# Sharing the first and last score columns of sliding-window attention in five tiles of the last layer, splitting the last tile's value products, and a new planned order

## The chip, the cores and the metric

The kernel runs on one core of one Trainium2 chip. The metric is the device time of one execution in microseconds (us), taken as the median of several runs. Five engines work side by side, each through its own queue in order: PE (TensorE, matrix products into PSUM), ACT (ScalarE, here the exponentials and some copies), DVE (VectorE, elementwise work), POOL (GpSimd, small work and some masks) and SP (SyncE, which issues DMAs). Semaphores join them.

## The reference: four layers, two kinds

`x` has 2048 tokens of width 512. Layers alternate: A (linear attention), B (causal attention over a window of 256 keys), A, B. Each adds its result to `x`. Heads: 32 of width 16. Cut to what matters here, the B layer is:

```python
scores = einsum("bhqd,bhkd->bhqk", q, k) * 16 ** -0.5
idx = arange(2048)
mask = (idx[:, None] - idx[None, :] >= 0) & (idx[:, None] - idx[None, :] < 256)
p = softmax(where(mask, scores, -1e9))
o = einsum("bhqk,bhkd->bhqd", p, v)
x = x + o.reshape(B, S, D) @ wo
```

A key at position n is seen by the queries n to n + 255 and no other.

## The kernel before: tiles, blocks of keys, and an order out of a table

All work is cut into 16 tiles of 128 tokens, numbered 0 to 15 (the change's "tiles ten to fourteen" are numbers 9 to 13). The program first records every operation with what it reads and writes (class `Plan`); then `place` takes the order of all operations, the engine of those that could run on either of two, and the PSUM bank of each result from a packed table (`TABLE`). So nothing is scheduled at run time: each engine runs its part of that list in order, and waits where a result or a bank isn't ready. Stages: layer 1 (A), layer 2 (B), layer 3 (A) and layer 4 (B); the code calls B's passes `middle(2)` and `middle(3)`, and interleaves the end of one layer with the start of the next.

In a B layer a tile j of keys is two blocks, b = 0 and 1, of 64 keys. Keys lie on the partitions of a score tile (64 keys times 2 heads = 128 partitions), queries on its columns. A block of 64 keys meets 64 + 255 queries, held in 320 columns:

- columns 0 to 255 are made by `b_scores` (line 617): eight matmuls for two head groups f (line 634) into four PSUM banks, then two exponentials on ACT of 128x1024 elements (line 644, one per pair of banks), then a causal mask on the first 64 columns on DVE (line 652);
- columns 256 to 319 are made by `b_far` (line 708) for all head groups of the tile at once: 32 matmuls of 64 columns (line 723), two exponentials of 128x1024 (line 732), and by `far_masks` (line 695) two masks, each on POOL (line 703) or on DVE (line 704).

So a tile takes ten exponentials of 1024 columns; tiles 14 and 15 have no far columns and fewer near ones, as the queries end. `b_values` (line 738) multiplies the probabilities with the values: 24 matmuls per head group (line 753), six blocks of keys for each of four, after the last block that reaches the tile. DVE divides by the sums (lines 765 and 766), the result is transposed, by a DMA or in the last tile by PE (line 789), multiplied with `wo` (line 400, last tile 800), added to `x` (line 568, last tile 806) and written out. The projections q, k and v of tile j + 3 are moved out of PSUM by ACT or DVE as the table says (`bqe`, `bve` at line 389, `bke` at 585 and 586).

A PSUM bank is held until its last reader is done. A group of scores needs four of the eight banks; usually two of them are freed by the first exponential of the group before, and the matmuls run while ACT works on that group's second.

The method `b_edge` (line 660), which does the shared columns, and the set `PACK` are in the kernel before already, with `PACK` empty.

Of the kernel before, what the change touches and what calls it, by code (L numbers as in the profile page):

```python
# [214 lines left out]
LATE = 5  # L215
KEEP = 6
MASKS = 0
PACK = {}
QUAD = ()
SUMMED = ()  # L220
FILL = 10
# [7 lines left out]
class Plan:  # L229
# [508 lines left out]
    def b_values(self, j, h, key):  # L738
        K = self
        rp = self.rp  # L740
        ps = Tile(1, K.cls)
        blocks = [(2 * j, 0), (2 * j + 1, -64), (2 * j - 1, 64), (2 * j - 2, 128), (2 * j - 3, 192), (2 * j - 4, 256)]
        blocks = [(b, c) for b, c in blocks if b >= 0]
        reads = []
        for f in (2 * h, 2 * h + 1):
            def put(e, f=f):
                m = None
                for gq in range(4):
                    r = 4 * f + gq
                    u = 4 * (f - 2 * h) + gq  # L750
                    for i, (b, c) in enumerate(blocks):
                        o = 384 * (b % 2) + c
                        m = e.matmul(K.ps(ps)[:, 34 * u:34 * u + 34], K.P((b // 2) % rp)[:, gq, f, o:o + P], K.vB[:, (b // 2) % 4, b % 2, r, :], start=i == 0, stop=i == len(blocks) - 1)  # L753
                return m
            rd = []
            for i in range(max(0, j - 2), j + 1):
                rd += [("P", i % K.rp, f)] + [("vB", i % 4, a, b) for a in range(2) for b in range(2)]
                rd += [("P", i % K.rp, f, b, h_) for h_ in range(3) for b in (0, 1)]
            rd += [("A", i % K.rp) for i in range(max(0, j - 2), j + 1)]
            if j >= 2:  # L760
                rd += [("F", (j - 2) % K.rp, h_) for h_ in (0, 1)] + [("F", (j - 2) % K.rp, h_, 1) for h_ in (0, 1)]
            self.pe("pv", put, key - 0.001 * (f % 2), 4 * len(blocks), 34, rd=rd, ps=[ps])
        s = j % 2
# [49 lines left out]
    def middle(self, ph):  # L813
        K = self
# [9 lines left out]
        self.packed = PACK.get(ph, ())  # L824
        if last:
# [59 lines left out]
    r"q*|$7s?a*Wo~3T8S1PT(rNZdAdWFiZPN~}}oerXQtJ5mI-lf87)baEk6;9t(XH*7Fy0I#tU#pC|pk_T=WzuKW9Cc3_{YJ&tqKByjx`2AChN~v3rY@-7sS)bF",
    r"s-;J&@cO+fq$B9kYLxn@N~nlBvo5TQ=t%m5imbEfggUEsDv{2ntxl}7>nJ*jE~=C2LaLZ{y0}iJE2|PZs!py;>Iy1{4z5b+e5$rCtb(bEx{l7N>*?XTk}j>A",
    r">&m){uA)|{7P_jgrbp=Nx`uA4SF5_Zl4_;bsHVD|ZmgT>J*u2)qZ{fby1s6$%d5Srfj+0!sz$o4KCddOeQKm$r$*`h>VlfBtE<s^j=rc4=`p&b`lPC=HF~U`",
    r"s}JjO`m>s+$Lj}bf_|tDsEK;MKBC*}NqT`^t1qdAdYWFOzo_YYonEXTsmZ#7e&c57y?TmXuV?Cxx|9B@rs`RGgWjh*>y7%d-mkmp<$9BTtXAmFdWn9bw&<05",
    r"ss5&}=w-UA4gy#8QGG)Pg=_kj?xu^uDt$~BhhT71AJ+%;6CFgK&`<SAy;YZhQ+k_zrh~%{9aJCG+x2t3Q<sEb`nrChcj?tSD!kOuAOr;0r644n)*<vOeMX0Z",
    r"(hwT%=;&}(hk<jthPtQE>xb@wzN@?IG7t}X=!^OkB!JVfN0)`_@LI=*a&QJ>K@GUAW5WoD2{mCP#DV*|HY9_D@J7GYF(5fS(C_p^Jqj-A6gmZ@)Q|LT9T&>O",  # L890
    r"d!0%@)~TQZeATISY8VY+Asmc>G>}G*g$NKHB0@zN2X$aPoP|U%0qQ~}hy;nD9-M=ox)!v6^N<88LsDo37hon_gjtXhT0&a*rY}Ji_^xL|1NfoSK_f^HKlN>B",
    r"2(96R&HxJP!ySkW8b0ZaFcI!Tc9;YJA9Wj;440uDTmgi}Ku|`1(QTouz6zNj3Y62Ibq>e^)gUJ{fvS)TGDB0C2hAWG<c2A*0H#8D&5#G?Lj|1|3^a#mS|A@R",
    r"ghh}QrolB>4A&t)SSSGPA-cW+OP~Wd=m;_NQdk9@Af{dhYhVt<(#v5kbcWT?ORs>Quo8Ofb+7^Y>4H!Q`s(!%2K(r+xE2b-6W9o^-7_cxn;;x+hNAEk!s7?1",
    r"h#%oORKhK=6?(xZsEoVe0Yt#wPz4`CM9ii8z<tQABjF?H3teCu&VZ_zM@Pon*bg2<6zm3Zu|MS1(=ng!3IiY>R>OgC2WQ|Qh>z9r4b;Fr&>h~wUbqK$u?O_m",
    r"@1Q2`gKaQCZ-*B!9bUp`*a5fTJ?w{McoV)r3OoR>;42)2*RTtc<4jD1QE{M7g5Mw-?u73!7@{L$VjKeLa3~ytx|k5tV+<Syvv4@X#MzhuQ(`8ZgGsR-X2w)l",
    r"A5&u%jD^kdFtos|SPPFpMy!o#uqCF&)>sD#+aO~ryocGaEgJj**)a~z#h=g!6JQQ(j5$%EU}roEO|T0tN5E!y47#Gm6__8pqs8OU4qv#H*dBZ0JiL!5paVX@",
    r"lh6YluEE&Y5er}t?1byEAojwC_|gT%ZnzeM;Rbw!y|EB(#6Gwln_^*n<u>7C%!Ng;FD}BO*bj5#V%&@ku^7(B;+O}Q;0`Q-3vd^{!G-u1^WjcxfP-{!9IS_6",
    r"UVMikaF~AULgF4AqE}-A+KZvEBo5W3a36-ogw!8P<4|0R1F#GZ!$h<SpWr|&i_7pSCZ;3!47cELJc?U!HzuJGcnp)$S8Ph#a6cxa@7Rn+Vsd(p%_#*9#&7rn",
    r"4`2&=iKFl%wxl0;5I^H~9F41J5FWx$xS9^*7(~iQt!OMVWun%UlG+f_8v1~#C=GqV%ybeB39Y5nbR5%?rJwj7(~+WA=;#EtrEH|>6awX-(>M;Z(-|C(K`0kZ",
# [194 lines left out]
```

## Time and profile before

| what | value |
|---|---|
| median of 3 runs | 417.3 us |
| lowest and highest | 416.35 and 420.33 us |
| the profiled execution, its own time | 415.97 us |
| its span | 414.2 us |
| mean granted TensorE clock | 0.999 of full speed |
| busy share of PE, DVE, ACT, POOL | 94%, 84%, 83%, 28% |

The page of the profile gives the busy time of each engine over the span, the busy share in 40 slices, the DMA queues, the chain of work that ended last, and groups of like instructions. A share over the whole span is a mean over stages with different limits; so the stages are looked at one by one. "ACT pb L644" is an instruction of ACT that writes the tile pb and was issued at line 644. `pb` and `vp` hold the probabilities of different tiles.

### The profile page before, as it was taken

The numbers are of one execution on the slowest core, as the hardware profiler recorded it, in microseconds if no ns is written. First come the engines' busy times: TensorE is split into PE (matmuls) and PEld (weight loads), VectorE is DVE, ScalarE is ACT, GpSimd is POOL, SyncE is SP. The second block draws the span as 40 slices with busy tenths as digits, with TensorE's granted clock in tenths as the row PEclk, the third lists the DMA queues.
The fourth block names the chain that finished last, engine by engine and source line by source line (L and its number), as shares of the span: only waits on it lengthen the run. The fifth ranks groups of instructions, "written<-read, shape, count | busy, mean of one in ns | idle before, by whom it ended". The sixth has DMA issues, their size and how long they took to land.

```text
span 414.2 us, 17130 instructions
## 1 busy us (share of the span) xinstructions
PE 387.9 (94%) x7481; PEld 258.5 (62%) x7555; DVE 346.8 (84%) x803; ACT 345.8 (83%) x432; POOL 117.7 (28%) x211
## 2 busy tenths in 40 slices
PE   7999999999999999999999999999999989988886
PEld 3545676766575577565666777586757745556554
DVE  5997898989989988778978689989799687776575
ACT  2624449998999999999997245999999999999992
POOL 4784833111241243230112302220132215230111
PEclk9999999999999999999999999999999999999999
DMA  7545316632233624444213100353306623273361
GB/s 246 177 79 148 104 40 119 131 92 68 64 96 78 110 73 113 80 107 106 56 29 69 26 2 27 93 148 79 81 7 134 137 56 95 60 159 96 93 121 54
DMA packets 67555, 37.83 MB, mean 91 GB/s; under 512 B 48248, under 2 KB 62584, under 8 KB 67480
## 3 DMA queue, kind: packets, MB, share of 16 engines
q1 hardware_dynamic: 67040, 35.54, 36.7%
q8 instruction: 60, 0.98, 1.0%
q0 software_dynamic: 432, 1.18, 0.9%
q14 instruction: 15, 0.12, 0.1%
q10 hardware_dynamic: 8, 0.00, 0.0%
HBM read 6.29 MB, written 2.10 MB: 20 GB/s over the span
## 4 chain that ended last, share of the span: by engine, by line
PE 48%; ACT 35%; DVE 9%; DMA 5%; issue 2%; SPq 1%
ACT pb L644 22%; PE ps L400 17%; PE ps L414 13%; PE ps L753 7%; ACT pb L732 6%; ACT vp L644 5%; PE ps L634 5%; PE ps L475 2%; DMA XQ<-xn 2%; DVE stats L361 2%; DMA xres<-in_A_x_dram 2%; DVE xres L568 1%; DVE XQ L557 1%; PE ps L723 1%; ACT vp L732 1%
## 5 line engine op out<-in xcount | busy, mean ns | idle before, releaser
L644 ACT ACTIVATE pb<-ps 128x1024 bf16<-128x1024 f32 (+2 forms) x224 | 206.7, 1042 | 4.5 <-PE ps L634 3.7
L753 PEld LDWEIGHTS ps<-vB,pb 128*128 128x128 bf16 x2560 | 77.5, 96 | 11.7 <-issue 4.6
L753 PE MATMUL ps<-vB,pb 128*128 128x34 bf16 x2560 | 83.2, 177 | 1.1 <-ACT pb L644 0.6
L414 PE MATMUL ps<-xT,wBp 128*128 128x128 bf16 x1024 | 69.2, 219 | 1.2 <-DVE vp L586 0.5
L414 PEld LDWEIGHTS ps<-xT,wBp 128*128 128x128 bf16 x1024 | 59.2, 98 | 13.6 <-issue 4.4
L423 ACT ACTIVATE tE<-ps 128x512 bf16<-128x512 f32 x64 | 38.5, 612 | 34.3 <-PE ps L400 15.5
L363 POOL TENSOR_SCALAR ve<-mv 128x1 f32<-128x1 f32 x64 | 16.7, 261 | 172.6 <-DVE mv L362 170.5
L634 PE MATMUL ps<-XQ,kB 32*128 32x256 bf16 (+2 forms) x1024 | 49.6, 267 | 5.0 <-ACT vp L644 1.4
L732 ACT ACTIVATE pb<-ps 128x1024 bf16<-128x1024 f32 x50 | 49.6, 1066 | 0.4 <-PE ps L723 0.2
L568 DVE TENSOR_TENSOR xres<-ps,xres 128x512 bf16<-128x512 f32 x63 | 43.1, 685 | 7.6 <-PE ps L400 7.0
L400 PE MATMUL ps<-wA,XQ 128*128 128x512 bf16 x176 | 46.2, 379 | 2.7 <-issue 0.6
L652 DVE TENSOR_TENSOR pb<-pb,tri 128x512 bf16<-128x512 bf16 x112 | 44.7, 412 | 4.0 <-ACT pb L644 3.7
L703 POOL TENSOR_SCALAR_AFFINE_SELECT pb<-pb 128x1024 bf16<-128x1024 bf16 x26 | 29.8, 1148 | 62.9 <-DVE pb L652 32.6
L361 DVE BATCH_NORM_STATS2 stats<-xres 128x6 f32<-128x512 bf16 x64 | 43.6, 686 | 2.6 <-DMA xres<-in_A_x_dram 1.8
L364 POOL TENSOR_TENSOR rs<-ve,negh 128x1 f32<-128x1 f32 x64 | 37.8, 591 | 5.3
L634 PEld LDWEIGHTS ps<-XQ,kB 32*128 32x128 bf16 x1024 | 15.5, 92 | 33.6 <-ACT pb L644 9.2
L414 PE MATMUL ps<-XQ,wA 128*128 128x128 bf16 x512 | 34.7, 219 | 0.3 <-DVE o L766 0.3
L414 PEld LDWEIGHTS ps<-XQ,wA 128*128 128x128 bf16 x512 | 30.4, 98 | 5.7 <-DVE o L766 0.6
L400 PE MATMUL ps<-wBv,xT 128*128 128x512 bf16 x112 | 31.5, 380 | 2.2 <-issue 1.3
L400 PE MATMUL ps<-wBo,oT 128*128 128x512 bf16 x105 | 28.8, 380 | 4.2 <-issue 1.1
L400 PE MATMUL ps<-M,XQ 128*128 128x512 bf16 x112 | 30.7, 380 | 2.1 <-issue 1.0
L765 DVE RECIPROCAL rc<-ps 128x16 f32<-128x16 f32 x64 | 16.1, 252 | 19.3 <-PE ps L753 19.0
(110 smaller groups left out, 532.8 us busy)
## 6 DMA issues: line engine op xcount, KB each, us to landing
vB<-vS SPq DMA_DIRECT2D x64, 136.0 KB, 2.6
kB<-vp SPq DMA_DIRECT2D x64, 128.0 KB, 2.7
wA<-in_A_wqkv_dram SPq DMA_DIRECT2D x3, 512.0 KB, 4.6
out_dram<-xres POOLq DMA_DIRECT2D x9, 128.0 KB, 2.8
xres<-in_A_x_dram SPq DMA_DIRECT2D x2, 512.0 KB, 4.3
pb<-in_B_wqkv_dram SPq DMA_DIRECT2D x1, 1024.0 KB, 5.6
xres<-in_A_x_dram SPq DMA_DIRECT2D x3, 256.0 KB, 4.8
out_dram<-xres SPq DMA_DIRECT2D x6, 128.0 KB, 2.4
```

Of the source, the lines that this page charges most:

```text
L361: self.on("DVE", "stats", lambda e: e.bn_stats(K.stats[:, t, :], K.xres[:, t, :]), key, dve(512), rd=[("xres", t)], wr=[("stats", t)])
L364: self.pow = self.on("POOL", "pow", lambda e: e.tensor_tensor(K.rs[:, t, :], K.ve[:, t, :], K.negh[:], ALU.pow), key + 0.03, (640, 690), r ...
L400: m = e.matmul(K.ps(ps), lhs(c), rhs(c), start=c == 0, stop=c == 3)
L414: m = e.matmul(K.ps(ps)[:, f * P:(f + 1) * P], w(c, f), xT(c), start=c == 0, stop=c == 3)
L423: self.on("ACT", "E", lambda e: e.activation(K.tE[:, s, :], K.ps(ps), ACT.Exp, bias=0.0), key, act(512), wr=[("tE", s)], ps=[ps])
L568: self.on("DVE", "res", lambda e: e.tensor_tensor(K.xres[:, t, :], K.ps(po), K.xres[:, t, :], ALU.add), key, dve(512), rd=[("xres", t)], w ...
L634: m = e.matmul(K.ps(ps[gq])[:, ns * i:ns * i + ns], K.kB[rows, j % 4, 2 * f + b, :, :], K.XQ[rows, f, q:q + ns], start=True, stop=True, ti ...
L644: return e.activation(out(2 * h, 2, ns), i, ACT.Exp, bias=0.0, scale=0.25)
L652: return e.tensor_tensor(x, x, K.tri[:, 0, sh:64].unsqueeze(1).unsqueeze(1).to_broadcast([P, 4, n, 64 - sh]), ALU.mult)
L703: return e.affine_select(out=x, in_=x, compare_op=ALU.is_ge, fill=0.0, base=-2, pattern=[[0, 16], [-2, 64]], channel_multiplier=1)
L732: return e.activation(far(h), i, ACT.Exp, bias=0.0, scale=0.25)
L753: m = e.matmul(K.ps(ps)[:, 34 * u:34 * u + 34], K.P((b // 2) % rp)[:, gq, f, o:o + P], K.vB[:, (b // 2) % 4, b % 2, r, :], start=i == 0, s ...
```

## The change

1. In the last layer, for tiles 9 to 13 (`PACK = {3: [9, 10, 11, 12, 13]}`), `b_scores` starts its 256 columns at 32 instead of 0, so it makes columns 32 to 287, and its mask covers 32 columns (operation `md`). `b_edge` takes the place of `b_far`: it computes columns 0 to 31 and 288 to 319 of both blocks. Only the first 32 keys of a block can meet the first 32 columns, and only the last 32 the last ones; so DVE copies partitions 64 to 127 of the last columns over the first ones, inside PSUM (`gc`, two copies of 512 elements), ACT takes exponentials of 128x512 elements twice instead of 128x1024, and DVE writes the first columns' part back to its place under a mask (`ma`, 64 partitions of 1024). The two far masks stay, on columns 256 to 319.
2. In the last tile (`SPLIT = {3: (15,)}`) the 24 value matmuls of each head group are recorded as two operations: 16 on earlier blocks of keys (`pu`) and 8 on the tile's own two blocks (`pv`).
3. A new `TABLE`: order, engines and banks of all operations in all layers. `HALF` is empty, so the third form in `b_values` (`ph`) isn't built.

```diff
-MASKS = 0
-PACK = {}
+PACK = {3: [9, 10, 11, 12, 13]}
+HALF = {}
+SPLIT = {3: (15,)}
...
-        blocks = [(2 * j, 0), (2 * j + 1, -64), (2 * j - 1, 64), (2 * j - 2, 128), (2 * j - 3, 192), (2 * j - 4, 256)]
+        blocks = [(2 * j, 0), (2 * j - 1, 64), (2 * j - 2, 128), (2 * j - 3, 192)]
+        ends = [(2 * j - 4, 256), (2 * j + 1, -64)]
+        apart = j in self.halves
+        if not apart:
+            blocks += ends
...
+        early = j in self.split
+        if early:
+            blocks = [x for x in blocks if x[1] <= 0]
+            before = [(2 * j - 1, 64), (2 * j - 2, 128), (2 * j - 3, 192), (2 * j - 4, 256)]
+            for f in (2 * h, 2 * h + 1):
...
+                self.pe("pu", put, key - 0.002 - 0.001 * (f % 2), 16, 34, rd=reads([f], before), ps=[ps])
...
 TABLE = (
...
```

`b_edge`, which now runs, is unchanged but first used:

```python
for h in range(2):
    two = ps[2 * h:2 * h + 2]
    side = lambda c, two=two: bass_view(K.PS[64:128, two[0].banks[0], c:c + 32], [[512 * (two[1].banks[0] - two[0].banks[0]), 2], [64, 8], [1, 32]])
    self.on("DVE", "gc", lambda e, side=side: e.tensor_copy(side(0), side(32)), key, dve(512), ps=two)
    def ex(e, h=h, two=two):
        return e.activation(edge(h), K.pair(two, [[128, 4], [64, 2], [1, 32]]), ACT.Exp, bias=0.0, scale=0.25)
...
def ma(e):
    x = lambda c: bass_view(K.P(sl)[0:64, 0, 0, c:c + 32], [[704, 16], [384, 2], [1, 32]])
    return e.tensor_tensor(x(0), x(288), K.tri[0:64, 0, 0:32].unsqueeze(1).unsqueeze(1).to_broadcast([64, 16, 2, 32]), ALU.mult)
```

What the new table moves, by operation counts. ACT to DVE: four evictions of v in layer 2 and one of q in layer 4, and one transposed tile in layers 1 and 2 each. DVE to ACT: two Gram-matrix evictions between layers 1 and 2, and one transposed half tile at the very end. Far masks on POOL: 15 to 19 in layer 4 and 14 to 15 in layer 2; on DVE 13 to 9 and 14 to 13. The counts of DMAs on SP and POOL stay.

In the list of layer 4, what each group of shared columns waits for is this. In tiles 9, 10 and 12 its banks come free with the first exponential of the pair just ahead on ACT's queue, so one exponential of 1024 columns runs while the group is made; in tiles 11 and 13 two do. In tile 15 the first group's banks are those of the last exponential of tile 14, and the third group's those of the exponential just ahead: none runs meanwhile there. In the table before, every group of the last eight tiles has one running. In layer 2 there are three groups with none before and six after (tile 8, tile 13's far columns and two more in tile 15 are new; tile 13 before had another).

More of the change, by code (lines that the diff above doesn't have):

```diff
@@ L215 @@
 LATE = 5
+MASKS = 0
 KEEP = 6
-MASKS = 0
-PACK = {}
+PACK = {3: [9, 10, 11, 12, 13]}
 QUAD = ()
 SUMMED = ()
+HALF = {}
+SPLIT = {3: (15,)}
 FILL = 10
@@ L824, in middle @@
         self.packed = PACK.get(ph, ())
+        self.halves = HALF.get(ph, ())
+        self.split = SPLIT.get(ph, ())
         if last:
@@ L885 @@
[L885 to L892, printed above, removed]
@@ new lines @@
+    r"t9PkeDwH~@rmGOTw5p+ls#B__zO81cGU|@1sCKHEDx^NG(&$k7m71l_sI)q?j;Hgedn$~ct@5g{`n5`@jn1dvDAeh7ejQ)GRd-bZO*(@fs@|!BdYH<oSZCB9",
+    r"l<48=y(*-`=@F{19;p)O{3^Vzr2|wY6+tJ|PDRw2bRr!|7f_kC)roZ$T|_6*1yxa<RY%svbT(Z`CDl$B*HLr{T}~y_Ido-JO4ru8RArrA*VScJC0$ZC)5TN;",
+    r"T~V)8<yCWCMOW3;^e|mrx6rFp9o<r|R>O4@-9|UkP4#ZIM%B}e^;%U$omKU91KmoWQ`J;M-B#~WBXn!MS5;6W^?7w)jncF9Y&}|kRCDwvHAe4KtMyzxRzFY|",
+    r")Hr=m&(q`ee0@moR}=IaeONEh6LoRbPCrx&^(4JkFVa(Wdp%80))&=uy+<F>9rRv3MbFUdbVt2U&(w?cBeh<4(fjohy+JS2o%B+@Q7_je)MvFxU(%iRX1zjR",
@@ L934 @@
+    r"L{}j5e)qkCrNA-`%ozkulh;JXmu(D8lD|$oWIroJ6qtT*slNq&Mh9PCiGP`w6MvBg#^y!rZ;QZqe3j#`L$4<SE7Nbs-!~pI1jgZ8?%jB4^0$#Mcy0WdQ{eOA",
+    r"e*h25L~Q",
 )
```

135 lines of the change are left out of this document (78 added, 57 removed).

## The prediction

> **What bounds the kernel now.** I read the page first, then busy time by stage, then the chain of waits of the last 75 us.
>
> ```profile
> span 414.2 us, 17130 instructions
> PE 387.9 (94%) x7481; PEld 258.5 (62%) x7555; DVE 346.8 (84%) x803; ACT 345.8 (83%) x432; POOL 117.7 (28%) x211
> PE 48%; ACT 35%; DVE 9%; DMA 5%; issue 2%; SPq 1%
> ```
>
> By the whole span PE seems to be the limit. The stages say otherwise. In the columns stand PE, its weight loads, DVE, ACT and POOL, each busy time with its count, then the granted clock (full almost throughout).
>
> ```profile
> 63.00:222.00 159.00, 152.16 (x3140) 101.26 (x3170) 139.15 (x327) 155.06 (x184) 37.81 (x67) 1.00 0.40 88
> 222.00:265.00 43.00, 42.08 (x660) 30.23 (x660) 37.53 (x83) 23.42 (x41) 9.90 (x18) 1.00 0.14 33
> 265.00:402.80 137.80, 126.92 (x2921) 86.63 (x2942) 108.84 (x247) 136.31 (x155) 31.74 (x47) 1.00 0.42 97
> 402.80:406.30 3.50, 3.50 (x108) 2.56 (x107) 3.12 (x9) 3.36 (x9) 0.54 (x1) 1.00 0.23 77
> 406.30:414.20 7.90, 3.83 (x83) 2.68 (x80) 3.41 (x10) 0.39 (x1) 0.54 (x1) 0.96 0.20 53
> ```
>
> In the two sliding-window layers, 63 to 222 and 265 to 402.8, ACT works 155.06 of 159 us and 136.31 of 137.8. The chain and ACT's longest waits confirm it: from 347 to 400 nothing but ACT stands in the chain, and ACT hardly waited.
>
> ```profile
> 346.97 12.84 ACT pb L644 x14
> 379.99 14.24 ACT pb L644 x16
> 397.90 1.83 ACT pb L732 x2
> ACT vp L644 <- PE ps L634: 0.6, 1, 0.6
> ACT pb L644 <- PE ps L634: 2.8, 8, 0.6
> ```
>
> (The fourth row is from 265 to 403, the last from 63 to 222: eight waits of 2.8 us in all.) So in these stages a microsecond off ACT ends the kernel one earlier, as long as PE and DVE keep delivering; 222 to 265, where ACT works 23.42 of 43, is not priced by it.
>
> **The change, part by part.** The prices of single instructions (columns: busy time of the group, mean ns of one); the first seven rows are ACT's, and its first row is from 63 to 222:
>
> ```profile
> L389 ACT ACTIVATE vS<-ps 128x512 bf16<-128x512 f32 x7 | 5.0, 708 | 0.0
> L732 ACT ACTIVATE pb<-ps 128x1024 bf16<-128x1024 f32 x22 | 21.9, 1075 | 0.1
> L732 ACT ACTIVATE vp<-ps 128x1024 bf16<-128x1024 f32 x6 | 5.8, 1036 | 0.1
> L644 ACT ACTIVATE vp<-ps 128x512 bf16<-128x512 f32 x4 | 2.1, 594 | 0.1
> L389 ACT ACTIVATE XQ<-ps 128x512 bf16<-128x512 f32 x2 | 1.2, 607 | 0.2 <-PE ps L414 0.2
> 376.22 1.94 ACT L644 ACTIVATE pb<-ps 128x1024 bf16<-128x1024 f32 x2
> 378.04 1.95 ACT L732 ACTIVATE vp<-ps 128x1024 bf16<-128x1024 f32 x2
> L652 DVE TENSOR_TENSOR pb<-pb,tri 128x512 bf16<-128x512 bf16 x22 | 8.6, 412 | 0.0
> L704 DVE TENSOR_TENSOR pb<-pb,tri 128x1024 bf16<-128x1024 bf16 x7 | 4.8, 687 | 0.3 <-ACT pb L732 0.3
> L389 DVE CAST vS<-ps 128x512 bf16<-128x512 f32 x6 | 4.1, 691 | 0.8 <-PE ps L400 0.8
> L703 POOL TENSOR_SCALAR_AFFINE_SELECT pb<-pb 128x1024 bf16<-128x1024 bf16 x4 | 4.6, 1152 | 1.7 <-DVE pb L652 1.5
> ```
>
> *Exponentials saved.* Two of ACT's run 1.94 us, yet the next starts 1.82 after the first: one follows another every 0.91 us and overlaps it by 0.12. The undisturbed 1036 ns row against the 594 ns row of 512 columns gives 0.44 us each; ten instructions (five tiles, two each) save 4.4 us on ACT.
>
> *The copies, and what they put in ACT's way.* Now a group of shared columns runs PE, DVE, ACT instead of PE, ACT. The times of that chain:
>
> ```profile
> 375.76 0.12 PEld L634 LDWEIGHTS ps<-XQ,kB 32*128 32x128 bf16 x8 [0.42 <-ACT vp L644]
> 377.51 0.41 PE L723 MATMUL ps<-XQ,kB 32*128 32x64 bf16 x32
> 379.12 0.12 PEld L634 LDWEIGHTS ps<-XQ,kB 32*128 32x128 bf16 x8 [0.22 <-ACT vp L732]
> ```
>
> The first L732 starts at 378.04, lasts some 1.03, and PE starts the group that waits for its banks at 379.12: 0.05 for the handover. Scores begun at 375.76 reach ACT at 376.22, shared columns begun at 377.51 at 378.04: 0.46 to 0.53. Count from the start of the exponential that frees the banks, with one more behind it (tiles 9, 10, 12): it ends at 1.03, PE starts at 1.08, DVE some 0.49 later at 1.57, the copy takes 0.69, ACT could start at 2.31, but is free at 1.82: 0.49 lost. The second copy ends 0.6 later, while ACT's short first exponential steps on after 0.47: 0.14 more. Together 0.65 per tile, 2.0 for three. In tiles 11 and 13 two exponentials (until 2.73) cover the copies; there only the next group of scores is late, as its cover is now a short instruction: 0.59 + 0.05 + 0.46 = 1.10 after the first short one starts, where ACT is done after 0.94. That is 0.16, 0.3 for both. Sum: +2.2 us. No copy from PSUM to PSUM stands in the trace. From below the 256-element divide bounds it (0.42 us, row at the tail), from above ACT's 1036 ns of twice the elements; I take the 691 ns cast, equal in elements and source. At the lower end the first copies gain 3 x 0.27 and the second cost nothing more (3 x 0.14): -1.2. At the upper end both copies of three tiles lose 0.35 each, and the second ones of tiles 11 and 13 also come late by 0.37: +2.8.
>
> *DVE and POOL.* A shared tile adds two copies (1.38) and the masked write-back of 1024 elements (0.69), and its four masks halve in columns, 0.41 to about 0.28, which the two mask rows give by their slope: +1.5 us, 7.7 for five. Four far masks go from DVE to POOL, -2.7 there and +4.6 here. Cover: DVE is idle 29 of 137.8 us, POOL 106. Priced at nothing; without the cover each is a delay of a copy, see the rivals. Behind a waiting copy stand DVE's evictions of q, k and v; who waits for those are the projections' DMAs, three tiles ahead. No DMA is added, and the output DMAs moved on SP and POOL come up long before the last rows.
>
> *The last tile's scores.* Its first group now waits for the last exponential of tile 14.
>
> ```profile
> 400.97 2.01 ACT L644 ACTIVATE pb<-ps 128x1024 bf16<-128x1024 f32 x2
> 402.12 0.24 PE L634 MATMUL ps<-XQ,kB 32*128 32x64 bf16 x8
> 402.78 3.50 ACT L644 ACTIVATE vp<-ps 128x256 bf16<-128x256 f32 x8
> 403.31 0.29 PE L634 MATMUL ps<-XQ,kB 32*128 32x128 bf16 x8
> 403.65 0.60 ACT L644 ACTIVATE vp<-ps 128x512 bf16<-128x512 f32 x1
> 403.58 0.77 PE L753 MATMUL ps<-vB,pb 128*128 128x34 bf16 x24
> 405.96 0.78 DVE L652 TENSOR_TENSOR vp<-vp,tri 128x512 bf16<-128x512 bf16 x2
> 407.17 0.42 DVE L766 TENSOR_TENSOR o<-ps,rc 128x256 bf16<-128x256 f32 x1
> 408.20 0.26 DVE L765 RECIPROCAL rc<-ps 128x16 f32<-128x16 f32 x1 [0.61 <-PE ps L753]
> ```
>
> Before, PE began it at 402.12 and ACT took it without a stop at 402.78, 0.20 ahead of its predecessor's end at 402.98. Now it can start 0.05 after that end, and 0.34 go by from PE's start to ACT's (403.31 to 403.65): 0.6 lost. The third group has no cover either, and stands on PE behind two value products (24 matmuls in 0.77 each): 0.5. Sum +1.1; 0.4 if PE is early, 1.6 if the products come late.
>
> *The last value products.* After the last mask (406.74) PE still had 48 of them before the reciprocal at 408.20. Now 32 of these run from the last exponential's end (402.78 + 3.50 = 406.28) under the mask, some 0.9 us at 24 in 0.67 (0.77 less the last one's latency), and 16 remain, 0.45: done at 407.7, so -0.5. Without this nothing else is late: the output products of tile 14 stand ahead, and their DMA lands earlier.
>
> *Layer 4's eviction.* One q goes from ACT to DVE: 607 ns less the overlap, -0.5.
>
> *Layer 2.* Four evictions of v leave ACT: 4 x (0.708 - 0.12) = -2.4; three more groups of scores have no exponential running while they are made, and the trace's waits of that kind reach 0.6: 3 x 0.5 = +1.5. Sum -0.9, between -2.4 (PE is early) and +0.6 (DVE, 88% busy here, delivers late).
>
> *The rest.* Other orders up to 63 us and from 222 to 265: the same work, two copies changed engine each way. No row favours a sign; zero, 1.5 either way.
>
> The sum: -4.4 + 2.2 + 1.1 - 0.5 - 0.5 - 0.9 = -3.0. The profiled execution took 415.97 us (span 414.2 and 1.8 around it): 413.0. It is 1.3 below the median, 417.3, and 0.4 below the lowest timed run; I leave the forecast at its level.
>
> [...] The copies start at partition 64, all else at 0. [...]
>
> **The rivals.**
>
> *The copies wait in DVE's queue.* DVE runs in order, with 0.69 us instructions about. Half of one ahead of each tile's first copy is 5 x 0.35 = 1.7, and layer 2 gains nothing (+0.9): 415.6. For it: DVE's load in the packed tiles rises by 1.5 us in each 9. Against: its idle time.
>
> *POOL's masks shut DVE's out.* If a select on POOL and a two-input mask on DVE exclude each other, a mask ahead of a copy waits up to 1.15 us: five tiles, 5.8, so 418.8. For it: eight of the ten far masks of shared tiles are on POOL. Against: most copies stand behind evictions, which read one tensor. [...]
>
> *Slower.* Every copy comes late by a whole queue: an eviction (0.69) and a mask (0.41) ahead of each of ten, and the four PSUM banks stay held meanwhile, so nothing else feeds ACT: 10 x 1.1 = 11 over the sum, 424. It decides from 0.85 us a copy, where 421.5 is passed. For it: the copies share the queue with evictions that wait for DMAs. Against: two of five tiles have 0.9 us to spare.
>
> *Better.* PE and DVE run ahead: the last tile loses 0.4 (-0.7), layer 2 keeps 2.4 (-1.5), the first stages give 1.5: 409.3. For it: only one wait over 0.5 in layer 4 before.
>
> That the change doesn't do what it says is excluded by the order: ten exponentials are of 512 columns.
>
> **How the numbers follow.** About 1% (4.2 us of 417.3) is what a measurement of this kernel can tell from no change: 413.1 and 421.5. The forecast, 413.0, lies at the lower edge; its own range is 411 to 414.3, of which 2.1 of 3.3 us lie below 413.1. Chances: forecast 0.46, better 0.18, queue 0.16, masks 0.04, slower 0.16. So of the forecast's 0.28 count as faster: faster 0.28 + 0.18 = 0.46; within 1% 0.18 + 0.16 + 0.04 = 0.38; slower 0.16. The range runs from a little below the better case to the masks' case, 408.8 to 418.8, and leaves out the slower case and some 0.04 of the better one.
>
> **What would show it.** Ten L734 rows of 128x512 near 0.59 us; copies of 0.69; ACT idle before the first shared exponential of tiles 9, 10 and 12 by about 0.5, and in 11 and 13 by none; ACT idle at the start of tile 15 by 0.4 to 0.6 twice; from ACT's last exponential to the end 7.4 us, not 7.9; ACT's busy time in layer 2 lower by 2.4 and the stage by 0.9. It is wrong if the first shared copies start more than 0.3 after their matmuls end, or if the stage from 222 to 265 or the first 63 us move by more than 1.5.

## The result, and the profile after

| | median of the runs | lowest to highest |
|---|---|---|
| before | 417.36 us | 416.01 to 420.33 |
| after | 415.86 us | 414.39 to 417.21 |

The ratio is 0.9962, 95% interval 0.9945 to 0.9979: faster by 1.5 us or 0.4%, within 1%. The forecast was 413.0, a fall of 3.0 us against the profiled execution and 4.3 against the median. Its range, 408.8 to 418.8, holds the time, but it would hold no change as well; the size of the fall does not stand. Executions whose mean granted clock is 0.996 or less take some 3 us longer (median 420.1 beside 416.9), 27 of 170 of the kernel before in the comparisons below and none of 32 of the changed kernel, so a part of the difference between the medians may lie there; without them the second comparison of the two (e13, below) has 0.85 us instead of 0.96.

The page of the changed kernel, span, busy times and the chain by engine:

```profile
span 415.4 us, 17157 instructions
PE 388.2 (93%) x7480; PEld 259.6 (62%) x7555; DVE 354.6 (85%) x817; ACT 341.3 (82%) x428; POOL 122.6 (30%) x216
PE 50%; DVE 21%; ACT 21%; DMA 3%; issue 3%; POOL 2%; POOLq 0%; DVEq 0%
```

ACT had 35% of the chain and has 21%; most of what it gave up went to DVE (9% to 21%). This execution took 417.21 us, the longest of the runs of after, while that of before took 415.97, shorter than any other. So the two traces differ by +1.2 us where the medians differ by -1.5, and their ends can't be compared; stages can. The same stretches as in the prediction (PE, weight loads, DVE, ACT, POOL):

```profile
63.00:222.00 159.00, 151.86 (x3134) 100.79 (x3168) 141.28 (x326) 152.53 (x180) 41.05 (x69) 1.00 0.39 90
222.00:265.00 43.00, 41.24 (x652) 29.93 (x657) 38.30 (x86) 21.90 (x39) 8.03 (x18) 1.00 0.13 33
265.00:402.80 137.80, 125.80 (x2890) 86.63 (x2911) 113.45 (x258) 134.47 (x154) 36.82 (x51) 1.00 0.39 95
402.80:406.30 3.50, 3.50 (x122) 3.02 (x122) 2.21 (x6) 2.33 (x5) 0.00 (x0) 1.00 0.52 120
406.30:414.20 7.90, 5.26 (x108) 3.45 (x106) 5.26 (x14) 2.51 (x6) 0.54 (x1) 1.00 0.30 85
```

In layer 2 (first row) ACT works 2.5 us less, as forecast, and waits instead. Its waits, the first three from 265 to 403, the last from 63 to 222 (where it was 2.8 in eight):

```profile
ACT pb L687 <- DVE ps L684: 1.1, 3, 0.4
ACT vp L646 <- PE ps L636: 0.8, 2, 0.6
ACT pb L646 <- PE ps L636: 0.3, 1, 0.3
...
ACT pb L646 <- PE ps L636: 3.2, 10, 0.6
```

L687 are the shared exponentials, L684 the copies. The new instructions (busy time, mean ns of one) cost what was put down for them, 705 beside 691 and 601 to 618 beside 594:

```profile
L684 DVE COPY ps<-ps 64x512 f32<-64x512 f32 x10 | 6.6, 705 | 1.4 <-PE ps L676 1.3
L687 ACT ACTIVATE pb<-ps 128x512 bf16<-128x512 f32 x8 | 4.7, 618 | 1.2 <-DVE ps L684 1.1
L687 ACT ACTIVATE vp<-ps 128x512 bf16<-128x512 f32 x2 | 1.1, 601 | 0.0
```

The timeline, on DVE at the copies of tile 10 and then at tile 12 (start, length, and in brackets the idle time before):

```profile
362.94 1.32 DVE L684 COPY ps<-ps 64x512 f32<-64x512 f32 x2
364.29 0.42 DVE L798 TENSOR_TENSOR o<-ps,rc 128x256 bf16<-128x256 f32 x1
...
381.00 2.00 ACT L646 ACTIVATE pb<-ps 128x1024 bf16<-128x1024 f32 x2
382.14 0.41 PE L676 MATMUL ps<-XQ,kB 32*128 32x64 bf16 x32
382.63 1.31 DVE L684 COPY ps<-ps 64x512 f32<-64x512 f32 x2 [0.46 <-PE ps L676]
383.38 1.20 ACT L687 ACTIVATE pb<-ps 128x512 bf16<-128x512 f32 x2 [0.38 <-DVE ps L684]
384.48 1.02 ACT L646 ACTIVATE pb<-ps 128x1024 bf16<-128x1024 f32 x1
```

PE ends at 382.55, DVE starts 0.08 later (0.08 in tiles 9, 10 and 13 too, 0.16 in tile 11): the copies don't stand in DVE's queue. ACT is idle 0.38 us before the first shared exponential, and without its usual overlap: from the start of the exponential just ahead to that of the shared one 1.47 us go by in tile 12 (381.91 to 383.38, the second of the two at 381.00), 1.60 in 9 and 1.45 in 10, where 0.90 is usual.

For the experiments I use lengths inside one trace, since most repeat to 0.2 us where whole times scatter by several; each length below is that of one trace. Spans are read to 0.1 us, so a tail is good to 0.05. "Tail" is the time from the start of tile 9's first exponential over block 0 (352.25 us before, 354.09 after) to the span's end, in three parts: to tile 15's first exponential, to the end of its last, to the end.

| run | parts | tail |
|---|---|---|
| before (three traces) | 50.53, 3.50, 7.92 | 61.95 (61.99, 62.02) |
| after (two traces) | 49.84, 4.24, 7.23 | 61.31 (61.46) |
| e1 late order only | 49.69, 4.24, 7.19 | 61.12 |
| e3 no sharing | 51.52, 4.24, 7.19 | 62.95 |
| e4 no copies | 48.66, 4.24, 7.18 | 60.08 |
| e7 no split | 49.82, 4.23, 7.82 | 61.87 |
| e8 cover in tile 15 | 49.06, 3.51, 9.00 | 61.57 |
| e9 direct scores | 50.64, 4.24, 7.20 | 62.08 |
| e14 two tiles | 50.63, 4.24, 7.26 | 62.13 |
| e15 cover in tile 12 | 50.02, 4.24, 7.22 | 61.48 |
| e16 both covers, first form | 49.42, 3.51, 9.02 | 61.95 |
| e17 tile 12, queue in order | 49.51, 4.24, 7.19 | 60.94 |
| e18 both covers, second form | 48.80, 3.51, 9.59 | 61.90 |

(The other traces of before are those of e6 and e5 below, which have its order here; the second of after is e13's. Four more traces have the order of before in the tail. e10's is 62.04, like the three. e2's is 62.44, with a last part of 8.18; e12's 62.74, with one of 8.72; e11's 64.21, with a granted clock of 0.99 from 265 to 402.8 us, where e10 and e12 have 1.00.) Against the four that agree the change wins 0.5 to 0.7 us in the tail, in e1's trace 0.8 to 0.9. All seven average 62.5, and the three with the change's late order 61.3: by these it is 1.2.

### The profile page after: what moved, and what is told of

Same layout as the page of the kernel before. It is cut to its first block, busy times and chain, and to the rows that moved or that the text cites. A ratio compares the mean times of both kernels' runs of the same rounds, so it can differ in the third digit from the quotient of the medians.

```text
span 415.4 us, 17157 instructions
## 1 busy us (share of the span) xinstructions
PE 388.2 (93%) x7480; PEld 259.6 (62%) x7555; DVE 354.6 (85%) x817; ACT 341.3 (82%) x428; POOL 122.6 (30%) x216
## 4 chain that ended last, share of the span: by engine, by line
PE 50%; DVE 21%; ACT 21%; DMA 3%; issue 3%; POOL 2%; POOLq 0%; DVEq 0%
PE ps L402 17%; ACT pb L646 13%; PE ps L416 12%; PE ps L783 9%; PE ps L636 5%; ACT pb L734 3%; DVE stats L363 3%; ACT vp L646 3%; DVE vp L427 2%; DVE xres L570 2%; DVE XQ L559 2%; DVE XQ L427 2%; DMA XQ<-xn 2%; DVE tE L426 1%; PE ps L477 1%
## 5 line engine op out<-in xcount | busy, mean ns | idle before, releaser
L646 ACT ACTIVATE pb<-ps 128x1024 bf16<-128x1024 f32 (+2 forms) x224 | 207.0, 1024 | 7.5 <-PE ps L636 6.4
L783 PEld LDWEIGHTS ps<-vB,pb 128*128 128x128 bf16 x2496 | 75.9, 96 | 12.7 <-DVE pb L654 2.9
L783 PE MATMUL ps<-vB,pb 128*128 128x34 bf16 x2496 | 81.3, 177 | 0.5 <-DVE mv L364 0.3
L705 POOL TENSOR_SCALAR_AFFINE_SELECT pb<-pb 128x1024 bf16<-128x1024 bf16 x29 | 33.2, 1145 | 59.2 <-DVE pb L654 19.4
L654 DVE TENSOR_TENSOR pb<-pb,tri 128x512 bf16<-128x512 bf16 (+1 forms) x112 | 43.8, 399 | 4.7 <-ACT pb L646 4.1
L734 ACT ACTIVATE pb<-ps 128x1024 bf16<-128x1024 f32 x42 | 41.4, 1057 | 1.1 <-PE ps L725 1.1
L416 PE MATMUL ps<-XQ,wA 128*128 128x128 bf16 x512 | 36.2, 219 | 0.4 <-ACT pb L646 0.3
L402 PE MATMUL ps<-wBv,xT 128*128 128x512 bf16 x108 | 30.3, 380 | 3.4 <-issue 1.6
L646 ACT ACTIVATE vp<-ps 128x1024 bf16<-128x1024 f32 (+2 forms) x32 | 26.8, 910 | 2.2 <-PE ps L636 2.1
```

The source lines that it names most:

```text
L402: m = e.matmul(K.ps(ps), lhs(c), rhs(c), start=c == 0, stop=c == 3)
L416: m = e.matmul(K.ps(ps)[:, f * P:(f + 1) * P], w(c, f), xT(c), start=c == 0, stop=c == 3)
L646: return e.activation(out(2 * h, 2, ns), i, ACT.Exp, bias=0.0, scale=0.25)
L654: return e.tensor_tensor(x, x, K.tri[:, 0, sh:64].unsqueeze(1).unsqueeze(1).to_broadcast([P, 4, n, 64 - sh]), ALU.mult)
L705: return e.affine_select(out=x, in_=x, compare_op=ALU.is_ge, fill=0.0, base=-2, pattern=[[0, 16], [-2, 64]], channel_multiplier=1)
L734: return e.activation(far(h), i, ACT.Exp, bias=0.0, scale=0.25)
```

## The experiments

My theory after the two traces: in the packed tiles ACT is the limit and the copies and lost cover hand back most of the saving; in layer 2 ACT is only one of several limits. The rival: the premise holds everywhere, and one trace misled me. Edits to the planned order are shown as the order of instructions.

**Which half of the kernel.** e1: the order of before until tile 9 of the last layer, then that of the change.

```diff
 order of before, entries 0 to 2223
-order of before, the rest;  PACK = {}, SPLIT = {}
+order of the change, the rest;  PACK = {3: [9, ... 13]}, SPLIT = {3: (15,)}
```

> The order of the kernel before up to tile 8's end of the last layer, and from tile 9's first scores on everything of the changed kernel: shared columns, split value products, new order. Theory (the two traces hold: the packed tiles cost what they save, 54.03 us before against 54.08 after, and the stretch behind the last exponential gains 0.7): 0.6 us under the kernel before, 416.8 beside 417.4. Rival (the whole measured gain of 1.5 us comes from these tiles, and the one trace is an unlucky run): 415.9. Forecast's own sum for this part: -4.4 + 2.2 + 1.1 - 0.5 = -1.6, so 415.8.

Measured 415.94 us beside 417.31, ratio 0.9972 (0.9937 to 1.0006); tail 61.12. e2 is the other half, cut in the middle of tile 8.

> The other half: the changed kernel's order up to the middle of tile 8 of the last layer, then the kernel before, nothing shared and nothing split. Theory (the rest of the measured -1.5 us lies here): 0.9 us under the kernel before, 416.5. Rival (these orders give nothing): 417.4. Second rival (the trace of after, which stands 1.8 us late at tile 9, is typical): 419.2.

Measured 418.22, ratio 1.0008 (0.9979 to 1.0038). In its trace 93.6 us lie between the last layer's first exponential and tile 9's, more than in any other trace (91.6 to 93.0), so it says only that the early orders bring no large gain: its interval leaves room for 0.9 us. By e1 the gain lies in the late part, though e1's interval just holds no change.

**Sharing, with and without its copies.** e3 takes the sharing out and leaves the order; e4 leaves only the copies out.

```diff
-PACK = {3: [9, 10, 11, 12, 13]}
+PACK = {}
```

> The changed kernel in its own order, without sharing: the ten exponentials have 1024 columns again, the ten copies and the five combining masks are gone, the masks have their full width. Theory (ACT is the limit in these tiles, so what the trace shows per instruction is what counts): 3.5 us of exponentials come back and 1.65 us of waits and lost cover go (three times 0.55), so 1.9 over the changed kernel, 417.7 beside its 415.9. Rival (PE and DVE would have ended no earlier, so shorter exponentials save nothing): 415.9, the same as the changed kernel.

Measured 417.85, ratio 0.9990 (0.9958 to 1.0022); tail 62.95. Sharing is worth 62.95 - 61.31 = 1.64 us (1.49 against the second trace).

```diff
-            self.on("DVE", "gc", lambda e, side=side: e.tensor_copy(side(0), side(32)), key, dve(512), ps=two)
```

> The changed kernel with the ten PSUM copies left out, so that the upper half of the shared columns holds other scores than it should; the exponentials are as short as in the change, and wait for PE alone. Theory (the copies put 0.5 us of waiting ahead of tiles 9, 10 and 12 and 0.15 more behind, nothing that another wait would take over): 1.6 to 1.9 us under the changed kernel, 414.1. Rival (the time returns as a wait for PE or for DVE's masks): 415.5 or more, within 0.4 of the changed kernel.

Measured 414.56, ratio 0.9943 (0.9914 to 0.9972); tail 60.08. Without copies the ten short exponentials give 62.95 - 60.08 = 2.87 us, and the copies take 1.23 of it (1.38 against the second trace).

**Layer 2.** e5 moves the four evictions alone.

```diff
-bve[layer 2: tiles 2, 4, 9, 10] on ACT
+bve[layer 2: tiles 2, 4, 9, 10] on DVE
```

> The kernel before, and in it only the four evictions of v of tiles 2, 4, 9 and 10 of layer 2 moved from ACT to DVE, as the change has them; order, banks and all else as before. The forecast's step (ACT is the limit in layer 2, so 4 x (0.708 - 0.12) goes): 2.4 us under the kernel before, 414.9 beside 417.3. Rival, formed from the trace of the changed kernel, in which ACT's freed time turned up as waits for PE: PE (152 of 159 us) and DVE (139, rising by 2.8) hold the layer together with ACT, and nothing is gained: 417 to 418.

Measured 418.17 beside 416.76, ratio 1.0034 (1.0014 to 1.0055): nothing gained, if anything lost. e6 was to shorten ten exponentials there.

> The kernel before, with ten of layer 2's far exponentials (tiles 9 to 13, two each) cut to 512 columns, so that the second half of their columns is left as an earlier tile had it; nothing is put in their place. This is the change's saving without its copies, in the other layer. If ACT is the limit there as it is in layer 4: 10 x 0.44 = 4.4 us under the kernel before, 412.9. Rival (PE or DVE is as late as ACT): under 1.5 us of it arrives, 416 or more.

Its edit did nothing: it chose the layer by a setting that is already the last layer's when instructions are written out, and all exponentials kept their length. So 416.60, ratio 1.0012 (0.9991 to 1.0033), is the kernel before once more. e10 is the same with the choice made in time. e11 instead leaves out the two farthest of the six blocks of keys in the value products of the same tiles, and e12 does both.

```diff
+w = 32 if self.rp == 3 and 9 <= j <= 13 else 64
-i = pair(ps[2 * h:2 * h + 2], [[128, 4], [64, 2], [1, 64]])
+i = pair(ps[2 * h:2 * h + 2], [[128, 4], [64, 2], [1, w]])
```

> The kernel before, with ten of layer 2's far exponentials (tiles 9 to 13, two each) really cut to 512 columns, the second half of their columns left as an earlier tile had it, and nothing put in their place: the change's saving without its copies, in the other layer. If ACT is the limit there, as its 155 of 159 us say: 10 x 0.43 = 4.3 us under the kernel before, 412.6 beside 416.9. Rival (PE, 152 of 159 us, is as late as ACT): under 2 us of it arrives, 415 or more.

```diff
+if self.rp == 3 and 9 <= j <= 13:
+    blocks = blocks[:4]
```

> The kernel before, with the value products of the same five tiles of layer 2 cut from six blocks of keys to four (the two farthest are left out), 5 x 4 x 8 matmuls less, some 0.2 us for each of 20 groups, 4 us of PE in all; ACT has all its work. If ACT is the limit in layer 2: nothing, 416.9. Rival (PE is the limit there): 3 to 4 us under the kernel before, 413.5. If both hold each other: 1 to 2 us.

> Both cuts of layer 2 together, 4.3 us of ACT and 4 us of PE. If either engine alone is the limit: the same as the run that cuts that engine. If the two are co-limits, so that each cut alone is taken up by the other engine: 3.5 to 4.3 us under the kernel before, 413, and more than the two cuts give one by one.

| run | time, ratio | from tile 2's first exponential to layer 2's last (starts) |
|---|---|---|
| before, e6, e1 (same order) | | 144.01, 144.15, 144.30 us |
| e5, evictions | 418.17 | 144.44 |
| e10, ACT 4 us less | 416.79, 0.9998 (0.9979 to 1.0018) | 143.79 |
| e11, PE 3 us less | 417.75, 1.0015 (0.9989 to 1.0040) | 143.69 |
| e12, both | 417.61, 1.0003 (0.9975 to 1.0031) | 143.40 |

Some 4 us off ACT bring 0.4, some 3 off PE 0.5, both 0.8 (against 144.15, the middle of the three, which differ by 0.3). The trace shows where it goes. The kernel before, timeline of ACT and of SP's queue:

```profile
71.97 1.36 SPq L594 DMA_DIRECT2D kB<-vp  x2
...
81.09 3.77 ACT L644 ACTIVATE pb<-ps 128x1024 bf16<-128x1024 f32 x4 [0.24 <-PE ps L634]
...
174.97 1.03 ACT L732 ACTIVATE pb<-ps 128x1024 bf16<-128x1024 f32 x1
175.88 0.62 ACT L389 ACTIVATE vp<-ps 128x512 bf16<-128x512 f32 x1
176.36 1.06 ACT L732 ACTIVATE pb<-ps 128x1024 bf16<-128x1024 f32 x1
177.26 5.68 ACT L644 ACTIVATE pb<-ps 128x1024 bf16<-128x1024 f32 x6
182.81 0.63 ACT L423 ACTIVATE tE<-ps 128x512 bf16<-128x512 f32 x1
```

The same of e10:

```profile
72.87 1.94 SPq L594 DMA_DIRECT2D kB<-vp  x2
...
83.48 3.78 ACT L644 ACTIVATE pb<-ps 128x1024 bf16<-128x1024 f32 x4 [1.73 <-PE ps L634]
...
177.39 0.61 ACT L734 ACTIVATE pb<-ps 128x512 bf16<-128x512 f32 x1
177.87 0.62 ACT L389 ACTIVATE vp<-ps 128x512 bf16<-128x512 f32 x1
178.35 0.63 ACT L734 ACTIVATE pb<-ps 128x512 bf16<-128x512 f32 x1
179.51 5.86 ACT L644 ACTIVATE pb<-ps 128x1024 bf16<-128x1024 f32 x6 [0.53 <-PE ps L634]
185.23 0.63 ACT L423 ACTIVATE tE<-ps 128x512 bf16<-128x512 f32 x1
```

From the first far exponential to the L423 behind the next groups: 182.81 - 174.97 = 7.84 and 185.23 - 177.39 = 7.84. Two exponentials shorter by 0.43, and not 0.01 us arrives: the next scores come when PE gets to them. PE is busy 7.79 of these 7.84 us in both traces (before, then e10):

```profile
174.97:182.81 7.84, 7.79 (x161) 5.48 (x161) 6.10 (x14) 7.84 (x11) 4.22 (x6) 1.00 0.45 116
```

```profile
177.39:185.23 7.84, 7.79 (x161) 5.48 (x161) 6.09 (x14) 7.17 (x11) 4.22 (x6) 1.00 0.52 121
```

With both cuts, the chain of waits runs through DVE alone from 194.5 to 203.6. Busy times from 63 to 222 in e12:

```profile
63.00:222.00 159.00, 149.42 (x2985) 97.71 (x3018) 139.19 (x328) 151.56 (x185) 38.74 (x67) 1.00 0.41 88
```

So ACT's 155 of 159 us did not make it the limit of layer 2. Nor is PE its only limit, since e11 and e12 gain little as well; what holds the rest stays open, as DVE's work and the planned order itself were not cut.

**The split.** e7 takes the early value products of tile 15 out and gives the late ones all their blocks.

```diff
-SPLIT = {3: (15,)}
+SPLIT = {}
```

> The changed kernel in its own order, the last tile's value products in one part again (the four early groups are taken out, the late ones have all their blocks). Theory (the early part runs under the last masks): 0.7 us over the changed kernel, 416.6 beside 415.9, and from ACT's last exponential to the end 7.9 us instead of 7.2. Rival (the end is set by the masks and the DMA, not by these products): 415.9, 7.2 unchanged.

Measured 416.07, ratio 0.9980 (0.9962 to 0.9999); tail 61.87, its last part 7.82 instead of 7.23: worth 0.4 to 0.6 us.

**Cover in the last tile.** e8 gives tile 15's scores other banks, ahead of tile 14's value products. With the banks, the first 16 of tile 15's early value products move as well, from ahead of tile 14's to behind tile 13's output products.

```diff
+scores 15, group 1 (banks 6,7 and 2,3)
 value products 14, f0
-scores 15, group 1 (banks 4,5 and 2,3)
-value products 14, f1
 scores 15, group 2
+value products 14, f1
```

> The changed kernel with the last tile's four groups of scores in other banks and earlier on PE, so that each is made while an exponential still runs; tile 14's value products and the output products of tiles 12 and 13 stand behind them, nothing is left out. Theory (the three waits of 0.54, 0.26 and 0.44 us that the trace shows ahead of tile 15's exponentials are the price of missing cover, 1.1 against 0.12 before): 0.8 to 1.1 us under the changed kernel, 414.9. Rival (PE, which worked without a stop in the last tile, is the limit there; what is made earlier makes the value products late, and the stretch behind the last exponential grows by as much): 415.9.

Measured 415.98, ratio 0.9983 (0.9962 to 1.0005). All three waits are gone, the last exponential ends 52.57 us after tile 9's first instead of 54.08, but the tail is 61.57: the last part grows by 1.8. Busy times in e8 until just before its last value products end, then in the changed kernel up to the same point:

```profile
401.00:408.60 7.60, 7.45 (x232) 5.93 (x231) 5.80 (x15) 4.38 (x10) 0.00 (x0) 1.00 0.36 81
```

```profile
401.60:409.50 7.90, 7.74 (x233) 6.34 (x234) 5.95 (x15) 5.28 (x10) 0.00 (x0) 1.00 0.42 100
```

PE is busy 98% in both. What ACT saves there only puts the same PE work behind the last exponential.

**Scores written in place.** e9 needs no copies:

```diff
-m = e.matmul(K.ps(ps[gq])[:, c:c + 64], K.kB[rows, j % 4, 2 * f + b, :, :], bass_view(K.XQ[rows, f, q:q + 32], [[288, 2], [1, 32]]), ..., tile_position=(32 * gq, 0))
+for g in range(2):
+    m = e.matmul(K.ps(ps[gq])[64 * g:64 * g + 64, c:c + 32], K.kB[rows, j % 4, 2 * f + b, 32 * g:32 * g + 32, :], K.XQ[rows, f, q + 288 * g:q + 288 * g + 32], ..., tile_position=(32 * gq, 64 * g))
```

> The changed kernel with the copies replaced: TensorE writes the first column's scores straight into the lower 64 partitions and the last column's into the upper 64 of the same PSUM columns, 64 matmuls of a 32 x 64 tile and 32 columns in place of 32 of 32 x 128 and 64 columns, so that the ten copies are gone and the output is whole. Theory (copies are what ACT waits for, and PE has room): between the run without copies and the change, PE paying up to 0.4 us for each of five groups: 414.6 to 415.5. Rival (64 small matmuls take twice the 0.41 us and PE, with 92% of these tiles, becomes the limit): 416 or more.

Measured 416.40, ratio 0.9976 (0.9954 to 0.9999); tail 62.08, 0.8 over the change and 2.0 over e4, which differs only in these matmuls. They take 3.4 us instead of 2.1 (from tile 9 to the last exponential, the changed kernel and then e9):

```profile
L676 PE MATMUL ps<-XQ,kB 32*128 32x64 bf16 x160 | 2.1, 189 | 1.3 <-DVE XQ L391 0.5 <-DVE xres L570 0.5 <-ACT pb L646 0.3
```

```profile
L677 PE MATMUL ps<-XQ,kB 32*64 32x32 bf16 x320 | 3.4, 189 | 1.3 <-DVE XQ L391 0.5 <-DVE xres L570 0.5 <-ACT pb L646 0.3
```

PE's extra 1.3 us cost at least as much time: here, too, PE has no room.

**The change again**, e13, without an edit.

> The changed kernel once more, beside the kernel before on one chip. Theory (from the traces: tiles 9 to 15 give 0.64, and the order up to there nothing but a rarer wait for a keys' transfer, 1.0 to 1.5 us in three of seven runs of the old order): 0.6 to 1.5 us under the kernel before. Rival (the first comparison was a lucky draw): within 0.3 of it. Its last tiles, from tile 9's first exponential to the end: 61.3 us again.

Measured 416.22 beside 417.18, ratio 0.9971 (0.9947 to 0.9994); tail 61.46.

**Sharing where the copies are covered.** e14:

```diff
-PACK = {3: [9, 10, 11, 12, 13]}
+PACK = {3: [11, 13]}
```

> The changed kernel with the columns shared in tiles 11 and 13 alone, whose copies run under two exponentials; tiles 9, 10 and 12 have their exponentials of 1024 columns back and no copies. Theory (in tiles 9, 10 and 12 the copies cost 0.55 to 0.70 and 0.13 us each of the 0.86 saved): the stretch from tile 9's first exponential to the end is 61.3 us plus 3 times 0.1, so 61.4 to 61.8, and the whole the same as the changed kernel. Rival (each shared tile brings the same): three fifths of the 1.64 us that sharing was found to give are lost, 62.3.

Measured 416.46, ratio 0.9974 (0.9952 to 0.9997); tail 62.13. Two covered tiles bring 62.95 - 62.13 = 0.82 us, 0.41 each; the three uncovered ones 0.67 to 0.82 more, a quarter each. Cover matters, but the tail lies nearer the rival's 62.3 than the theory's 61.4 to 61.8.

**Cover for tile 12.** e15 makes its shared scores one exponential earlier.

```diff
 scores 12, f2-3, b0
+scores 12, shared (banks 6,7 and 4,5)
 projections q and k of tile 15 (four groups of matmuls)
-scores 12, shared (banks 0,1 and 4,5)
 scores 12, f0-1, b1
```

> The changed kernel with tile 12's shared scores made one exponential earlier, in two banks that are free by then, so that two exponentials cover the copies as in tiles 11 and 13; the last projections move behind them. Theory (the missing cover is what the stall of 0.57 us ahead of tile 12's first shared exponential is): the stall is gone, and the stretch from tile 9 to the end is 0.4 to 0.6 shorter, 60.8. Rival (PE, which now has its projections later, gives it back): 61.3.

Measured 415.83, ratio 0.9959 (0.9937 to 0.9981); tail 61.48, no gain. The stall is gone, and another stands behind it (e15, ACT and PE):

```profile
381.43 1.16 ACT L687 ACTIVATE pb<-ps 128x512 bf16<-128x512 f32 x2
383.09 1.94 ACT L646 ACTIVATE pb<-ps 128x1024 bf16<-128x1024 f32 x2 [0.50 <-PE ps L636]
...
380.75 1.96 PE L416 MATMUL ps<-xT,wBp 128*128 128x128 bf16 x32 [0.30 <-ACT pb L646]
382.64 0.40 PE L636 MATMUL ps<-XQ,kB 32*128 32x256 bf16 x8
```

The projections, 1.96 us on PE, now stand between the two groups of scores. e17 puts the last quarter of them behind.

```diff
-q 15, k 15, k 15, q 15, scores 12 f0-1 b1
+q 15, k 15, k 15, scores 12 f0-1 b1, q 15
```

> The run with tile 12's copies covered, and one more step: of the four groups of projection matmuls (1.96 us together) that stood on PE between the shared scores and the next ordinary ones, the last (0.49) goes behind the ordinary ones, and the keys' eviction ahead of the queries'. Theory (the 0.57 us that cover took away came back as 0.50 because PE's queue, not ACT or the copies, made the next scores late): the wait behind tile 12's shared exponentials goes, and the stretch from tile 9 to the end is 61.0 us, 0.4 to 0.5 under the run before it (61.48). Rival (the next resource takes it up again): 61.3 or more.

The wait is gone (e17):

```profile
383.41 1.16 ACT L687 ACTIVATE pb<-ps 128x512 bf16<-128x512 f32 x2
384.62 1.94 ACT L646 ACTIVATE pb<-ps 128x1024 bf16<-128x1024 f32 x2
```

The tail is 60.94, the shortest of all whole kernels, 0.4 to 0.5 under the change. Measured 415.84, ratio 0.9945 (0.9920 to 0.9971); the kernel before took 418.54 beside it, 1.2 or more over the other comparisons, so the ratio flatters. Against the change's 415.86 and 416.22 it can't be told from it by whole times.

**Both covers.** e16 joins e8 and e15, with tile 13's output products behind the last value products; e18 joins e8's with e17, and puts tile 14's behind the last transposes.

```diff
-output products 13, value products 15, output products 14, transposes 15
+value products 15, output products 13, transposes 15, output products 14
```

> The same, and the last tile's scores covered too, with what stood in the way of the run that did only that put right: tile 13's output products come behind the last value products, and the last masks ahead of the sums and divisions of tile 14. Theory: tile 12's 0.5 us, and in the last tile 0.2 to 0.4 (the covered run lost 0.26 where tile 13's output products took 0.43 of PE before the end): 60.4 to 60.7 from tile 9 to the end, 0.7 to 0.9 us under the changed kernel. Rival (PE has the same work left at the last exponential in any order): 60.8 or more.

> Tile 12 covered with PE's queue in order (the run before), and the last tile's scores covered too, with tile 14's output products no longer ahead of the last transposes, where they waited for their transfer in the other run with both covers. Theory (in the last tile, too, what a covered exponential saves is there if PE's queue lets it through): the last tile's three waits are gone (1.4 us), PE has about 1.0 us more to do behind the last exponential; 60.5 us from tile 9 to the end, 0.4 under the run before (60.94). Rival (PE's work that is left sets the end in any order): 60.9 or more.

Measured 416.71, ratio 0.9975 (0.9950 to 1.0001), tail 61.95; and 416.73, ratio 0.9996 (0.9974 to 1.0018), tail 61.90. Both miss. In e18 the value products end 2.4 us after the last exponential (3.2 in e8, 1.4 in the change). Then PE is idle for 0.36 us, until ACT has moved a transposed half, and tile 14's output products, 0.9 us of PE, stand ahead of the last four. Three orders did not turn the last tile's cover into time; that none could is not shown.

## Why the prediction was wrong, step by step

**The bound.** "In these stages a microsecond off ACT ends the kernel one earlier" is the step that failed. In layer 2 it fails at once: four evictions off ACT bring nothing (e5), and 4 us of exponentials bring 0.4 (e10). The forecast read ACT's busy share and its short waits; PE worked 152.16 of the same 159 us, and 7.79 of 7.84 in the stretch shown of e10, where ACT's work was cut. In the packed tiles it holds in part: 10 x 0.43 = 4.3 us of shorter steps gave 2.87.

**Exponentials, -4.4.** A step is the time from the start of one exponential to the start of the next. It is 0.48 us after a short one and 0.91 after a long one, as forecast. But in e4 a third is lost again: the steps behind the five short pairs are 0.91, 0.68, 0.66, 1.09 and 0.70, so 1.6 us more than five times 0.48. Where the profile shows ACT idle there, it names PE, as behind tile 12's pair:

```profile
381.94 7.44 ACT L646 ACTIVATE pb<-ps 128x1024 bf16<-128x1024 f32 x8 [0.40 <-PE ps L636]
```

**Copies, +2.2.** The mechanism was right, in place too: idle 0.38 before the first shared exponential of tiles 9, 10 and 12, none in 11 and 13. By ACT's steps they cost 0.70 + 0.55 + 0.57 and three times 0.13 for the second copy, 2.2 in all. Another 0.15 and 0.22 go behind the short pairs of tiles 11 and 13, but e4 has 0.18 and 0.22 there without any copy: that is the shorter cover, as forecast. What failed is that the 2.2 would all be on the path. By e4 only 1.2 to 1.4 is: without copies PE makes ACT wait behind the pairs of tiles 9, 10 and 12 instead. The net of exponentials and copies, -2.2 forecast, is -1.5 to -1.6.

**Last tile's scores, +1.1.** Idle of 0.54, 0.26 and 0.44 where two waits were forecast; in steps about 1.5 us (the exponential ahead of the first takes 1.65 instead of 0.90 to the next, the tile's own exponentials 4.24 instead of 3.50). The waits:

```profile
403.93 0.66 ACT L646 ACTIVATE vp<-ps 128x256 bf16<-128x256 f32 x2 [0.54 <-PE ps L636]
404.85 1.08 ACT L646 ACTIVATE vp<-ps 128x512 bf16<-128x512 f32 x2 [0.26 <-PE ps L636]
406.37 1.80 ACT L646 ACTIVATE vp<-ps 128x512 bf16<-128x512 f32 x4 [0.44 <-PE ps L636]
```

The tail behind tile 15's first exponential is 11.47 us, before 11.42, and giving the cover back gained nothing. e3 prices the new late order without sharing: its tail is 1.0 over before's although the split gives 0.4 to 0.6 there, so 1.5 where the forecast had 1.1. Sharing, order and split together are the -0.5 to -0.7 of the tail; the forecast had -1.6. **Value products, -0.5:** right, -0.4 to -0.6 (e7).

**Layer 4's eviction, -0.5.** From the layer's first exponential to tile 9's, five traces of the old order take 91.6 to 91.8 us, twelve of the new 92.0 to 92.9: nothing gained (e11 and e12, of the old order, 93.0 and 92.9).

**Layer 2, -0.9.** From its first exponential to the last layer's, 197.3 and 197.5 us in the old order (before, e6), on average 197.5 in twelve traces of the new (196.4 to 198.5). Inside, the border moved: the new order's last exponential of layer 2 comes 1.9 us later on average, and the stretch from there to the last layer's first is 32.9 us where the old order has 34.6 to 34.9. So one sign of being wrong that the prediction named, a move by more than 1.5 in the stage behind layer 2, came true, and the sum hides it. e5 prices the evictions at zero or worse: the gain of 2.4 was not there. The +1.5 for missing cover was not tried by itself.

**The rest, zero.** On average it is zero, but one thing moved that I had not seen. In the old order the first scores of tile 2 in layer 2 wait for a keys' transfer in some executions: ACT is idle 1.73 us in e10 and 0.24 before (rows 83.48 and 81.09 above; the issues are those at 72.87 and 71.97). (The profile names that transfer in e5 and e10, a DVE instruction in e1.) SP's two issues took 1.80 to 1.94 us in the three traces with the wait, and 1.23 to 1.65 in the four without. From the layer's first exponential to that one it is 18.0 us in these four and 19.0 to 19.5 in the three; in thirteen traces of the new order 17.5 to 18.3. Three in seven times 1.0 to 1.5 us is 0.6 on average. But the new order gives it back elsewhere: from the start to tile 9's first exponential seven traces of the old order take 353.3 us on average (352.9 the three without an edit there), twelve of the new 353.2. So the rarer wait does not show as a gain, and e2 has none either. What the traces do show is the tail: 0.5 to 0.7 us against the four that agree, 1.2 by all, beside 1.5 and 1.0 measured. Which of the two is typical stays open. The profiled execution of before was one without the wait, 1.4 us under the median: a sum made against it starts too low.

**The rivals.** Copies queued on DVE: no, they start 0.08 to 0.16 us after their matmuls. That this rival's 415.6 lies next to the measured time is chance, though its other half, that layer 2 gains nothing, came true. POOL's masks: that a select and a mask of DVE exclude each other was the author's assumption; three masks are late under a select, below, and none of them ahead of a copy. The slower case: no copy was late by a queue. What comes behind the copies of tiles 10 and 13 reads PSUM and starts 0.03 us after their end (364.29 beside 362.94 + 1.32 = 364.26, 392.15 beside 390.81 + 1.31 = 392.12), where the second copy starts 0.09 before the end of the first; what holds it no run here shows. No exponential is late by it: the first copies start 0.08 us after PE in four of five tiles, and what comes behind the second one is none.

## What to carry to other kernels

An engine busy 155 of 159 us of a stage need not be its limit when another, busy 152, feeds it (layer 2 here). Look for the next instruction that depends on another engine: only if its start would move does a saving arrive. Test that by cutting the work alone before counting it. Where two engines hold each other, cover and queue have to be moved together (e15's tail of 61.48 us against e17's of 60.94). And take the level for a forecast from the median, with the trace for the differences.

## What the runs showed of the hardware

In two pairs of traces of one order (before and e6, the change and e13) 304 of 311 steps between exponentials agree to 0.02 us, and the others differ by up to 0.2. The wait for tile 2's keys above is a larger jump, 1.0 to 1.5 us.

A DVE mask of 128x1024 with two operands, usually 687 ns, took 1.21 us beside a select on POOL (timelines of DVE and of POOL in the changed kernel):

```profile
399.32 1.21 DVE L706 TENSOR_TENSOR pb<-pb,tri 128x1024 bf16<-128x1024 bf16 x1
```

```profile
398.85 1.15 POOL L705 TENSOR_SCALAR_AFFINE_SELECT pb<-pb 128x1024 bf16<-128x1024 bf16 x1 [2.31 <-DVE pb L654]
```

It ends 0.53 us after the select does, at 400.53 and 400.00. Twice more in this trace a mask starts under a select (at 130.99 and at 199.14, 1.15 us each) and is late: one of 1024 elements at 131.33 takes 1.33 us, one of 512 at 199.59 takes 0.97 instead of 0.42. What holds them no run here shows. The copies of tiles 10, 11 and 13, which read one operand and ran beside selects from 362.11, 373.22 and 390.73, kept their 0.7 us each.
